# A spectral filter and a maxout feed-forward layer: five visits in the last overlapped batch, and filter rows by way of fp32

## The chip, the cores and the metric

The kernel runs on one core of a Trainium2 chip. The metric is the device time of one execution in microseconds. The core has TensorE (matrix multiplication into PSUM), VectorE, ScalarE, GpSimd, and SyncE, which here only issues DMA transfers. GpSimd issues DMA transfers too.

## The reference

```
x: (8, 3072, 256)   filt_r, filt_i: (1537, 256)

X = rfft(x, axis=1)
y = irfft(X * (filt_r + 1j * filt_i), n=3072, axis=1)      # 8 x 3072 x 256

h1 = y @ w1          # 24576 x 1024
h2 = y @ w2
out = maximum(h1, h2) @ w_out
```

## The kernel before, in words

The transform over 3072 points is split into 96 x 32. A batch passes through four spectral stages: `s1` (a transform of length 96, into `ad` in DRAM, read back as `bt` by `s1_read`), `s2` (twiddles and the transform of length 32, into PSUM tiles `px`), the product with the filter `F` (`product`, tiles `pq`), `s3` (the inverse of length 32, PSUM tiles `pz`, evicted by ScalarE as `zt` and written to `zd` in DRAM, read back as `zr` by `z_read`) and `s4` (the inverse of length 96, giving `yt`). The feed-forward layer then works on tiles of 384 tokens, eight to a batch. It uses max(h1, h2) = max(h1 - h2, 0) + h2: `moe_h` multiplies by `Wd` = w1 - w2 into a PSUM tile `ph`, which VectorE or ScalarE evicts through a maximum with zero as `gt`; `moe_o` sums `gt` times `Wo` and `yt` times `M` = w2 w_out into `po`, evicted by VectorE as `ot` and written out by GpSimd's transfers.

The order is written out by hand. The main loop goes over tiles `tt`, eight steps `j` to each, so 64 steps to a batch. A step issues `moe_h` of this tile, then what the table `mid` holds for the step, then three or four matmul groups of `moe_o` of the tile before, then what the table `todo` holds. While batch b goes through the feed-forward layer, its table entries carry the spectral stages of batch b + 1 (and `s1` of b + 2 in the same visits). `mid` holds the visits: visit n of a batch does `s3` of part n - 1 (there are six parts), `s2` of part n and its two products on VectorE. `plan_f2` puts seven visits into each batch; for batches 2 to 6 they stand at steps 7, 14, 18, 24, 31, 38 and 42, and `z_read` three steps behind the fourth and the seventh. In batch 6 the visits work on the last batch, 7, and carry no `s1`; batch 7 has none. Of each tile VectorE evicts the `ph` of j = 1, 3 and 6, half of the `py` of `s4` and all `po`; ScalarE does the rest.

PSUM tiles `px`, `pz`, `ph`, `py` and `pa` share one pool of six buffers, `ps`, handed out in turn; `po` has two of its own. `pq` has six buffers, `zt` three.

The start-up runs batch 0 through the spectral stages by a path of its own (`s1t`, `t1`, `s3t`, `t2`) and builds the tables. The filter lies in `F`, 128 partitions by real and imaginary part, 12 places w, two s, 256 columns, in bf16. `load_f(h)` fetches the places of half h, in GpSimd's queue behind the eight loads of batch 0's `x`, with a cast from fp32 on the way: rows counted up in partitions 0 to 15 of each half, rows counted down in partitions 16 to 31. For k = 0 the second set is not a row counted down, so row 48 + 96 p comes with a transfer of its own (line 124). `double_f` copies partitions 0 to 31 of each half to 32 to 63: for h = 0 by four VectorE copies (line 130), for h = 1 by SyncE transfers. One row, partition 32 at place 0, is mended by `fix_f` with the last filter row, 1536, which `load_fn` fetches. Only the product of part 0 reads place 0.

Of the kernel before, what the change touches and what calls it, by code (L numbers as in the profile page):

```python
# [8 lines left out]
FP32 = mybir.dt.float32  # L9
# [4 lines left out]
B = 8  # L14
N = 3072
D = 256
# [10 lines left out]
def kernel(  # L27
# [14 lines left out]
    nc = tc.nc  # L42
    V, S, G, TE = nc.vector, nc.scalar, nc.gpsimd, nc.tensor
# [7 lines left out]
    F = const.tile([128, 2, NW, 2, D], BF16)  # L51
# [12 lines left out]
    XF = [const.tile([128, 2, 2, D], FP32, name="XF%d" % k) for k in range(3)]  # L64
# [7 lines left out]
    init = setup.enter_context(tc.tile_pool(name="init", bufs=1))  # L72
# [10 lines left out]
    def load_x(b, c, n):  # L83
        for k in range(c, c + n):
            xb[b, k] = x_tile(b, k)[0:NP]
        src = x[b].rearrange("(p m) d -> p m d", m=NM)
        m0 = 4 * (c % 2)
        G.dma_start(out=xb[b][0:NP, m0:m0 + 4 * n], in_=src[:, 4 * c:4 * c + 4 * n, :])
# [21 lines left out]
    def load_f(h):  # L110
        w0, w1 = WP[h]
        n = 2 * (w1 - w0)
        for g in range(2):
            for ri, f in enumerate((filt_r, filt_i)):
                k0 = 24 * g + 2 * w0
                src = bass.AP(f.tensor, f.offset + k0 * D, [[96 * D, 16], [D, n], [1, D]])
                G.dma_start(out=F[64 * g:64 * g + 16, ri, w0:w1].rearrange("p w s d -> p (w s) d"), in_=src)
                n0 = 1 if k0 == 0 else 0
                src = bass.AP(f.tensor, f.offset + (96 - k0 - n0) * D, [[96 * D, 16], [-D, n - n0], [1, D]])
                G.dma_start(out=F[64 * g + 16:64 * g + 32, ri, w0:w1].rearrange("p w s d -> p (w s) d")[:, n0:n],  # L120
                            in_=src)
                if n0:
                    src = bass.AP(f.tensor, f.offset + 48 * D, [[96 * D, 16], [1, D]])
                    G.dma_start(out=F[16:32, ri, 0, 0], in_=src)

    def double_f(h, g, ri, engine):
        w0, w1 = WP[h]
        o_, i_ = F[64 * g + 32:64 * g + 64, ri, w0:w1], F[64 * g:64 * g + 32, ri, w0:w1]
        if engine is V:
            V.tensor_copy(o_, i_)  # L130
        else:
            nc.sync.dma_start(out=o_, in_=i_)

    FN = init.tile([33, D], FP32)

    def load_fn():
        nc.sync.dma_start(out=FN[32:33], in_=filt_r[1536:1537, :])

    def fix_f():
        V.tensor_copy(F[32:33, 0, 0, 0], FN[32:33])  # L140


    V.memset(W1, 1.0)
# [21 lines left out]
    for q in range(2):  # L165
        G.memset(hv[:, q], 1.0)
        for r in (0, 32):
            G.memset(hv[r:r + 1, q], 0.5 * (1 - q))
    load_f(0)
    load_f(1)  # L170
    load_fn()
    load_x(1, 0, 2)

    def table_c():
# [196 lines left out]
    def s2(b, v):  # L371
        px = [ps.tile([128, 2, D], FP32, tag="ps", name="px%d" % s) for s in range(2)]
        for i in range(2):
            for s, g in ((0, 0), (1, 1), (0, 1), (1, 0)):
                u = 2 * (2 * v + i) + g
                TE.matmul(px[s][64 * g:64 * g + 64, i], U[64 * s:64 * s + 64, u], bt[b][64 * s:64 * s + 64, u],  # L376
                          start=True, stop=True)
        return px

    def product(E, v, s, px, pool=None):  # L380
        pq = (pool or pqpool).tile([128, 2, 2, D], BF16, tag="pq", name="pq")
        E.tensor_tensor(pq, px.rearrange("p (o i) d -> p o i d", o=1).to_broadcast([128, 2, 2, D]),  # L382
                        F[:, :, 2 * v:2 * v + 2, s], OP.mult)
        return pq
# [7 lines left out]
    def s3(b, v, pq):  # L392
        if v == 0:
            zd[b] = dram.tile([NU, 128, D], BF16, tag="zd", name="zd")
        pz = [ps.tile([128, 2, D], FP32, tag="ps", name="pz%d" % g) for g in range(2)]
        for i in range(2):
            for q, tab in enumerate((VP, VQ)):
                for g, s in ((0, 0), (1, 1), (0, 1), (1, 0)):
                    TE.matmul(pz[g][64 * s:64 * s + 64, i], tab[64 * g:64 * g + 64, 2 * v + i, s],  # L399
                              pq[s][64 * g:64 * g + 64, q, i], start=(q == 0), stop=(q == 1))  # L400
        zt = zpool.tile([128, 2, 2, D], BF16, tag="zt", name="zt")
        for g in range(2):
            S.activation(zt[:, :, g], pz[g], AF.Copy)  # L403
        nc.sync.dma_start(out=zd[b][4 * v:4 * v + 4].rearrange("u p d -> p u d"),
                          in_=zt.rearrange("p i g d -> p (i g) d"))

    pend = {}

    def visit(b, n, quads):
# [7 lines left out]
        if n < 6:  # L417
            pend[b, n] = [product(V, n, s, px[s]) for s in range(2)]

    yt = {}  # L420

    def s4(tt):
# [165 lines left out]
    for g in range(2):  # L588
        for ri in range(2):
            double_f(0, g, ri, V)  # L590
            if g == 0 and ri == 0:
                fix_f()
    xs = {}

    def stage_x(v):
# [69 lines left out]
    def plan(b, step, fn, *a):  # L665
        todo.setdefault((b + step // 64, step % 64), []).append((fn, a))
# [6 lines left out]
    mid = {}  # L673

    def plan_f2(b, steps, quads, xs, folds):
        for n, st in enumerate(steps):
            mid.setdefault((b, st), []).append((visit, (b + 1, n, quads[n])))
        plan(b, steps[3] + 3, z_read, b + 1, 0)
        plan(b, steps[6] + 3, z_read, b + 1, 1)
        if b + 2 < B:  # L680
            for c in range(8):
                plan(b, xs[c], load_xf, b + 2, c)
                plan(b, folds[c], fold, b + 2, c)
            plan(b, steps[-1] + (6 if b else 11), s1_read, b + 2)
# [5 lines left out]
    for c in range(2, 8):  # L690
# [1 line left out]
    plan_f1(0, 1, (5, 6, 7, 7, 10, 10, 11, 11, 12, 12, 13, 13), 14)  # L692
    plan_f2(0, (25, 28, 31, 35, 38, 42, 46), ((0,), (1,), (2,), (3,), (4,), (5,), (6, 7)),
            (8, 10, 15, 18, 21, 27, 30, 33), (16, 19, 25, 28, 31, 34, 38, 42))
    for b in range(1, B - 1):
        plan_f2(b, (7, 14, 18, 24, 31, 38, 42) if b > 1 else (14, 18, 24, 30, 34, 39, 42), ((0, 1), (2,), (3,), (4,), (5,), (6,), (7,)),
                range(-32, 32, 8) if b > 1 else range(-25, 31, 7), range(-22, 42, 8) if b > 1 else range(-15, 41, 7))

    for tt in range(8 * B + 1):
        b, i = divmod(tt, 8)  # L700
        k = 0
        for j in range(8):
            step = 8 * i + j
# [4 lines left out]
            if tt > 0:  # L708
                n = 3 if j in (3, 7) else 4
# [36 lines left out]
```

## Time and profile before

| | us |
|---|---|
| median of 3 runs (lowest, highest) | 503.55 (502.16, 515.77) |
| the profiled execution | 502.04 |
| its span, first to last instruction | 500.2 |
| TensorE busy in the span | 488.7 |
| VectorE busy | 331.4 |
| ScalarE busy | 308.6 |
| GpSimd busy | 259.7 |
| mean granted TensorE clock | 0.992 |

Busy time counts instructions in progress; those of TensorE overlap one another, so rows are read from start to start. Times in the views count from the start of the span. "L480" is line 480 of the kernel, and what follows "<-" in brackets is what ended an engine's idle time.

### The profile page before, as it was taken

The page shows a single profiled execution, that of the slowest core. Times are in us where ns is not written, and L with a number is a line of the kernel's source. Part 1 is how long each engine was busy: PE and PEld are TensorE (multiplying, and loading weights), DVE is VectorE, ACT ScalarE, POOL GpSimd, SP SyncE. Part 2 cuts the span into 40 slices and gives each one's busy share as a digit, 9 for nine tenths or more (in the row PEclk, how much of TensorE's full clock was granted, in tenths as well). Part 3 has the DMA queues.
Part 4 walks back from the last instruction along what each step waited for, and adds up shares of the span by engine and source line. Part 5 has one row for each costly group of instructions (what it writes and reads, how often), then busy time and mean ns, then how long its engine had stood idle before and what let it go on. Part 6 is the DMA issues. An engine that isn't in the chain of part 4 may idle for free.

```text
span 500.2 us, 13079 instructions
## 1 busy us (share of the span) xinstructions
PE 488.7 (98%) x5300; PEld 361.7 (72%) x5300; DVE 331.4 (66%) x514; ACT 308.6 (62%) x629; POOL 259.7 (52%) x342
## 2 busy tenths in 40 slices
PE   8699999999999999999999999999999999999996
PEld 4456767777777777777777777777777777777775
DVE  7786788458865786567755787457764687555552
ACT  6777478657764777557674677547774565544442
POOL 7894678548463954627654764637632221222220
PEclk9979999999999999999999999999999999999999
DMA  7999889996899668978789568896759236411112
GB/s 122 166 245 210 260 218 272 294 257 208 234 285 244 180 206 236 240 186 235 206 236 282 178 182 250 222 234 202 201 185 249 84 113 144 167 65 64 64 64 84
DMA packets 77981, 97.19 MB, mean 194 GB/s; under 512 B 8033, under 2 KB 54370, under 8 KB 77858
## 3 DMA queue, kind: packets, MB, share of 16 engines
q1 hardware_dynamic: 64658, 66.73, 51.4%
q0 software_dynamic: 13264, 29.64, 20.5%
q8 instruction: 41, 0.67, 0.6%
q14 instruction: 18, 0.15, 0.1%
HBM read 53.87 MB, written 47.19 MB: 202 GB/s over the span
## 4 chain that ended last, share of the span: by engine, by line
PE 93%; ACT 2%; DMA 1%; DVE 1%; POOL 1%; issue 0%; POOLq 0%
PE po L480 34%; PE ph L448 33%; PE po L478 8%; PE pz L399 5%; PE py L428 4%; PE pa L349 2%; PE px L376 2%; DMA xb<-in_x_dram 1%; PE pt L532 1%; PE pr L553 1%; PE pt L526 1%; PE pa L324 1%; ACT at L509 1%; DVE pq L382 0%; ACT bt L518 0%
## 5 line engine op out<-in xcount | busy, mean ns | idle before, releaser
L480 PE MATMUL po<-Wo,gt 128*128 128x256 bf16 x1536 | 261.0, 273 | 0.0
L452 ACT ACTIVATE gt<-ph 128x384 bf16<-128x384 f32 x321 | 157.2, 496 | 144.9 <-PE ph L448 144.2
L480 PEld LDWEIGHTS <-gt 128*128 128x128 bf16 x1536 | 146.6, 98 | 66.0 <-issue 10.3
L461 POOL DMA_DIRECT2D out_dram<-ot x186 | 103.0, 557 | 171.5 <-DVE ot L492 168.9
L450 DVE TENSOR_SCALAR gt<-ph 128x384 bf16<-128x384 f32 x191 | 105.0, 554 | 64.0 <-PE ph L448 62.0
L382 DVE TENSOR_TENSOR pq<-px,F 128x1024 bf16<-128x1024 f32 x91 | 107.0, 1220 | 23.3 <-PE px L376 22.7
L448 PEld LDWEIGHTS <-Wd 128*128 128x128 bf16 x1024 | 96.5, 98 | 12.1 <-issue 0.5
L103 POOL TENSOR_TENSOR xb<-XF 128x512 bf16<-128x512 f32 x48 | 61.3, 1276 | 53.1 <-PE py L428 24.3
L492 DVE COPY ot<-po 128x512 f32<-128x512 f32 x95 | 65.2, 686 | 25.1 <-PE po L480 24.0
L104 POOL TENSOR_TENSOR xb<-XF 128x512 bf16<-128x512 f32 x48 | 61.1, 1273 | 0.0
L353 ACT ACTIVATE at<-pa 128x512 bf16<-128x512 f32 x96 | 51.8, 608 | 2.4 <-PE pa L349 2.1
L403 ACT ACTIVATE zt<-pz 128x512 bf16<-128x512 f32 x84 | 45.6, 594 | 11.8 <-PE pz L399 9.7
L428 PE MATMUL py<-G,zr 96*128 96x96 bf16 x512 | 32.7, 206 | 0.4 <-DVE zr L556 0.3
L428 PEld LDWEIGHTS <-zr 96*128 96x128 bf16 x512 | 28.9, 97 | 3.0 <-DVE zr L556 1.0
L399 PE MATMUL pz<-pq,VP 64*64 64x256 bf16 x336 | 22.2, 281 | 0.1
L376 PE MATMUL px<-bt,U 64*64 64x256 bf16 x384 | 20.2, 277 | 1.2 <-ACT VQ L273 0.7
L399 PE MATMUL pz<-pq,VQ 64*64 64x256 bf16 x336 | 21.0, 269 | 0.0
L399 PEld LDWEIGHTS <-VP 64*64 64x64 bf16 x336 | 9.8, 105 | 13.6 <-issue 13.3
L349 PE MATMUL pa<-xb,CT 64*64 64x512 bf16 x192 | 19.5, 383 | 0.0
L376 PEld LDWEIGHTS <-U 64*64 64x64 bf16 x384 | 10.5, 108 | 4.1 <-issue 3.8
L563 PE MATMUL pd<-W 128*128 128x512 bf16 x28 | 10.2, 488 | 1.5 <-DVE zero L145 1.5
L349 PEld LDWEIGHTS <-CT 64*64 64x64 bf16 x192 | 8.7, 105 | 2.1 <-ACT gt L452 1.2
(429 smaller groups left out, 606.3 us busy)
## 6 DMA issues: line engine op xcount, KB each, us to landing
out_dram<-ot POOLq DMA_DIRECT2D x186, 128.0 KB, 3.5
XF<-in_x_dram SPq DMA_DIRECT2D x96, 192.0 KB, 5.1
ad<-at SPq DMA_DIRECT2D x56, 192.0 KB, 3.7
zd<-zt SPq DMA_DIRECT2D x42, 256.0 KB, 2.6
zr<-zd SPq DMA_DIRECT2D x56, 192.0 KB, 5.0
bt<-ad SPq DMA_DIRECT2D x13, 768.0 KB, 9.8
WS<-in_moe_w_dram SPq DMA_DIRECT2D x4, 512.0 KB, 7.1
xb<-in_x_dram POOLq DMA_DIRECT2D x8, 192.0 KB, 5.9
```

Source lines behind the costliest of these rows:

```text
L103: G.tensor_tensor(t_[:, 0], f[:, 0], f[:, 1], OP.add)
L104: G.tensor_tensor(t_[:, 1], f[:, 0], f[:, 1], OP.subtract)
L353: S.activation(at[:, m0:m0 + 2], pa[g], AF.Copy)
L382: E.tensor_tensor(pq, px.rearrange("p (o i) d -> p o i d", o=1).to_broadcast([128, 2, 2, D]), F[:, :, 2 * v:2 * v + 2, s], OP.mult)
L399: TE.matmul(pz[g][64 * s:64 * s + 64, i], tab[64 * g:64 * g + 64, 2 * v + i, s], pq[s][64 * g:64 * g + 64, q, i], start=(q == 0), stop=(q ...
L428: TE.matmul(py[:, m], zr[b][:, 4 * i + m, 128 * dc:128 * dc + 128], G1, start=True, stop=True)
L448: TE.matmul(ph, Wd[:, dc, 128 * j:128 * j + 128], y_[:, dc], start=(dc == 0), stop=(dc == 1))
L450: V.tensor_scalar(gt[tt][:, j], ph, 0.0, None, OP.max)
L452: S.activation(gt[tt][:, j], ph, AF.Relu)
L461: E.dma_start(out=dst, in_=ot[tt // 2][:, 3 * (tt % 2) + c])
L480: TE.matmul(p_, g_[:, n - 2, blk], Wo[:, n - 2], start=(e == 0), stop=(e == 9))
L492: V.tensor_copy(ot[tt // 2][:, e - 1:e + 1], po[q // 2 % 2])
```

## The change

Batch 6 gets a table of its own, `LAST`, with five visits at steps 7, 13, 21, 29 and 37 in place of seven at 7, 14, 18, 24, 31, 38 and 42. The visits do `s2` of parts 0 and 1; `s3` of 0 and `s2` of 2 and 3; `s3` of 1 and 2 and `s2` of 4; `s3` of 3 and 4 and `s2` of 5; `s3` of 5. The products of a visit's parts follow its `s2`. `z_read` of batch 7 moves from steps 27 and 45 to 24 and 40.

In the start-up, the filter rows that belong to place 0 of the first half (rows 96 p and 96 p + 48, of both parts of the filter) are fetched by SyncE in fp32 into an `XF` tile that is not yet in use, with row 1536 behind them; GpSimd writes the first four sets, cast to bf16, into `F` ahead of its F loads. `load_f` leaves place 0 out and no longer issues line 124. `fix_f` takes row 1536 from the same tile and stands behind the fourth VectorE copy instead of the first.

```diff
         for g in range(2):
+            n0 = 1 if h == 0 and g == 0 else 0
+            k0 = 24 * g + 2 * w0 + n0
             for ri, f in enumerate((filt_r, filt_i)):
-                k0 = 24 * g + 2 * w0
-                src = bass.AP(f.tensor, f.offset + k0 * D, [[96 * D, 16], [D, n], [1, D]])
-                G.dma_start(out=F[64 * g:64 * g + 16, ri, w0:w1].rearrange("p w s d -> p (w s) d"), in_=src)
-                n0 = 1 if k0 == 0 else 0
-                src = bass.AP(f.tensor, f.offset + (96 - k0 - n0) * D, [[96 * D, 16], [-D, n - n0], [1, D]])
-                G.dma_start(out=F[64 * g + 16:64 * g + 32, ri, w0:w1].rearrange("p w s d -> p (w s) d")[:, n0:n],
-                            in_=src)
-                if n0:
-                    src = bass.AP(f.tensor, f.offset + 48 * D, [[96 * D, 16], [1, D]])
-                    G.dma_start(out=F[16:32, ri, 0, 0], in_=src)
+                for r0, o, step in ((0, k0, D), (16, 96 - k0, -D)):
+                    src = bass.AP(f.tensor, f.offset + o * D, [[96 * D, 16], [step, n - n0], [1, D]])
+                    o_ = F[64 * g + r0:64 * g + r0 + 16, ri, w0:w1].rearrange("p w s d -> p (w s) d")
+                    G.dma_start(out=o_[:, n0:n], in_=src)
...
-    FN = init.tile([33, D], FP32)
+    FZ = XF[0][0:33, 0]

     def load_fn():
-        nc.sync.dma_start(out=FN[32:33], in_=filt_r[1536:1537, :])
+        for ri, f in enumerate((filt_r, filt_i)):
+            for q in range(2):
+                src = bass.AP(f.tensor, f.offset + 48 * q * D, [[96 * D, 16], [1, D]])
+                nc.sync.dma_start(out=FZ[16 * q:16 * q + 16, ri], in_=src)
+        nc.sync.dma_start(out=FZ[32:33, 0], in_=filt_r[1536:1537, :])
+
+    def put_fz(ri):
+        G.tensor_copy(F[0:32, ri, 0, 0], FZ[0:32, ri])

     def fix_f():
-        V.tensor_copy(F[32:33, 0, 0, 0], FN[32:33])
+        V.tensor_copy(F[32:33, 0, 0, 0], FZ[32:33, 0])
...
+    load_fn()
+    for ri in range(2):
+        put_fz(ri)
     load_f(0)
     load_f(1)
-    load_fn()
...
+    LAST = (((), (0, 1)), ((0,), (2, 3)), ((1, 2), (4,)), ((3, 4), (5,)), ((5,), ()))
+
+    def visit_last(b, n):
+        for v in LAST[n][0]:
+            s3(b, v, pend.pop((b, v)))
+        px = {v: s2(b, v) for v in LAST[n][1]}
+        for v in px:
+            pend[b, v] = [product(V, v, s, px[v][s]) for s in range(2)]
...
             double_f(0, g, ri, V)
-            if g == 0 and ri == 0:
-                fix_f()
+    fix_f()
...
-    for b in range(1, B - 1):
+    for n, st in enumerate((7, 13, 21, 29, 37)):
+        mid.setdefault((B - 2, st), []).append((visit_last, (B - 1, n)))
+    plan(B - 2, 24, z_read, B - 1, 0)
+    plan(B - 2, 40, z_read, B - 1, 1)
+    for b in range(1, B - 2):
         plan_f2(b, ...
```

## The prediction

> **What bounds the kernel now.** I read the page's busy table and clock row first, then the chain that ended last, and then the timelines of TensorE, VectorE and GpSimd around the two places that the change touches: the start-up (0 to 32 us) and batch 6 (steps 0 to 63, about 388 to 444 us).
>
> ```profile
> PE 488.7 (98%) x5300; PEld 361.7 (72%) x5300; DVE 331.4 (66%) x514; ACT 308.6 (62%) x629; POOL 259.7 (52%) x342
> PE 93%; ACT 2%; DMA 1%; DVE 1%; POOL 1%; issue 0%; POOLq 0%
> ```
>
> TensorE is the bound: 98% busy and 93% of the chain. All else costs time only where it makes TensorE wait. In batch 6 it has no gap. TensorE around the first two visits of batch 6 (start, duration, instructions):
>
> ```profile
> 393.88 0.49 PE L448 MATMUL ph<-y__7128,Wd 128*128 128x384 bf16 x2
> 394.30 0.41 PE L376 MATMUL px<-bt,U 64*64 64x256 bf16 x8
> 394.64 0.50 PE L480 MATMUL po<-Wo,gt 128*128 128x256 bf16 x3
> ...
> 399.78 0.49 PE L448 MATMUL ph<-y__7192,Wd 128*128 128x384 bf16 x2
> 400.20 0.30 PE L399 MATMUL pz<-pq,VP 64*64 64x256 bf16 x4
> 400.33 0.28 PE L399 MATMUL pz<-pq,VQ 64*64 64x256 bf16 x4
> 400.44 0.28 PE L399 MATMUL pz<-pq,VP 64*64 64x256 bf16 x4
> 400.55 0.28 PE L399 MATMUL pz<-pq,VQ 64*64 64x256 bf16 x4
> 400.66 0.39 PE L376 MATMUL px<-bt,U 64*64 64x256 bf16 x8
> 400.98 0.61 PE L480 MATMUL po<-Wo,gt 128*128 128x256 bf16 x4
> ```
>
> Read start to start, since durations overlap. A ph pair normally takes 0.33 us (431.17 to 431.49 in the same view); before a visit it takes 0.42 (399.78 to 400.20). Eight px take 2 x 0.11 = 0.22 at the rate of the pz rows, and 0.32 where the next work is 128 rows wide (400.66 to 400.98). So a visit pays about 0.1 on entering and 0.1 on leaving: 0.2 us of TensorE time.
>
> VectorE in the same stretch:
>
> ```profile
> 394.75 2.36 DVE L382 TENSOR_TENSOR pq<-px,F 128x1024 bf16<-128x1024 f32 x2 [0.55 <-PE px L376]
> 397.03 0.68 DVE L492 COPY ot<-po 128x512 f32<-128x512 f32 x1
> 397.62 1.01 DVE L450 TENSOR_SCALAR gt<-ph 128x384 bf16<-128x384 f32 x2
> 399.22 0.56 DVE L434 TENSOR_SCALAR y__7286<-py 128x384 bf16<-128x384 f32 x1 [0.58 <-PE py L428]
> ```
>
> A product is 1.22 us, the second of a pair 1.14 later; the evictions behind it are next in VectorE's queue. The evictions behind a pair are done at 398.63, and VectorE then waits 0.58 us: that slack, some 0.6 us a visit, hides each pair today.
>
> **Part 1, batch 6: five visits.** Same matmuls, products and evictions; only their places change. Two visits fewer save 2 x 0.2 = 0.4 us of TensorE. Against it, visits 0 and 1 (steps 7 and 13) now queue four products each in one block. Four take 3 x 1.14 + 1.22 = 4.64 us, in which VectorE evicts nothing. I follow the queues from the first visit with the starts above; the second px set moves TensorE 0.22 later.
>
> Products end at 395.97, 397.11, 398.25, 399.39. Behind them stand ot (to 400.0), gt of step 9 (400.47), gt of step 11 (400.93), y (401.4). PSUM pool ps has six buffers handed out in turn: after four px, step 10's ph takes the first px, step 11's the second, step 12's the third, the first py the fourth, and step 13's ph the buffer of step 9's. With 0.1 us for a release to reach TensorE (an estimate from the start gaps of the rows):
> - step 12's ph: due 397.92 + 0.22 = 398.14, free 398.35: stall 0.2.
> - py: due 398.68 + 0.42 = 399.10, free 399.49: stall 0.4.
> - step 13's ph: due 399.02 + 0.8 = 399.8, free 400.57: stall 0.75.
>
> The second visit then needs six buffers at once (two pz, four px); step 11's gt holds one for 0.1 more. TensorE is through at about 402.0, VectorE begins four more products there, and ends them at 406.6; an ot and the gt of step 14 follow, ready at 407.8. Step 18's first po reads that gt (column 6 of the tile before). TensorE gets there at about 405.9: step 14 starts at 402.45, steps last some 0.76, and step 18's ph waits 0.25 for a px buffer. Stall 0.25 + 1.85.
>
> By then VectorE catches up: visits at steps 21, 29 and 37 bring 2, 2 and 0 products, as many as a visit has now, so I cost them at nothing; the cover is the same 0.6 us. The pairs of pz at steps 21 and 29 give ScalarE four zt of about 0.55 us (400.88 to 401.97 for two in its timeline), 1.1 more in a row than now; with about 1 us idle before its gt rows this is hidden, and uncovered it would cost 0.5. The z reads go out at steps 24 and 40 instead of 27 and 45, and are wanted at step 62: nothing.
>
> Sum for batch 6: 0.2 + 0.4 + 0.75 + 0.1 + 0.25 + 1.85 = 3.55, less 0.4: **+3.1 us**. Bounds: the saving alone, -0.4; and, if the two products that each block of four brings early are exposed in full (4 x 1.14 = 4.6) and the 0.6 us of cover fails at steps 21 and 29 as well (1.2), +5.8.
>
> **Part 2, the filter rows.** GpSimd's queue at the start:
>
> ```profile
> 7.34 0.22 POOL L168 MEMSET hv<- 1x1 f32 x2
> 7.58 0.49 POOL L117 DMA_DIRECT2D F<-in_filt_r_dram  x1
> 8.07 0.58 POOL L120 DMA_DIRECT2D F<-in_filt_r_dram  x1
> 8.65 0.49 POOL L124 DMA_DIRECT2D F<-in_filt_r_dram  x1
> 10.00 0.49 POOL L117 DMA_DIRECT2D F<-in_filt_i_dram  x1 [0.86 <-DMA xb<-in_x_dram]
> ```
>
> Removed: two L124 issues, 1.0 us. Added ahead of the first F issue: two 32x256 copies. The nearest GpSimd copies are 0.26 us (48x96) and 1.05 (128x1024); I take 0.35 each, 0.7. They wait for SyncE's rows: SyncE issues five transfers from 0.75 at 0.36 each, done by 2.6; its transfers on the page land 2.6 to 9.8 us later, so at 5.2 to 12.4 against GpSimd's arrival at 7.56. Most likely no wait (16 KB each, where 9.8 is for 768 KB and 2.6 for 256); at worst 4.8 us. Queued behind are all F loads and load_x(1, 0, 2). The fourth issue waits for an x load until 10.0 anyway, which takes up a delay of 0.9 us. VectorE's copies of F begin at 18.43, behind bt; the second F issue, whose rows the first copy needs, moves from 8.07 to about 8.8, and with the longest landing of its line (7.3 us) is there at 16.1, 2.3 early. So: nothing; at worst 12.4 + 0.7 + 0.5 + 7.3 = 20.9, 2.5 late.
>
> The 64 KB travel ahead of x, which is on the chain (6.17 us of DMA from 4.68). At the 122 to 166 GB/s of the page's first two slices that is 0.4 to 0.5 us if all of it delays x, and nothing if the DMA engines are idle, as they are until about 2.3; F issues 0.7 later give some back. I take **+0.2**, from -0.5 to +0.5.
>
> **Part 3, the mended row** moves from between VectorE's first and second F copy to behind the fourth. Its 0.28 us is in the same unbroken run (18.43 to 23.73), so VectorE ends alike: nothing. GpSimd's first product, at 23.91, now waits for it and starts alike. The second set, F loads for h = 1, moves two places up, about 1 us; its SyncE copies and the w loads follow, with their users busy elsewhere: nothing.
>
> Sum: 502.04 (the profiled execution: span 500.2 plus 1.8 around it) + 3.1 + 0.2 = **505.3 us**. That execution lies 0.3% under the shown median of 503.55 and near its lowest, 502.16. A measurement tells about 2% here, 10 us, so I expect no decided difference.
>
> **Rivals.** (a) *The blocks are absorbed*: if releases come quicker or the buffers go round otherwise, only the visits saved count: 502.04 - 0.4 = 501.6, not slower. For it: VectorE is busy 66% over all. Against: the gt of step 14 is behind the second block in a queue that is in order. It decides if that gt is ready by 405.9. 0.15.
>
> (b) *The clock drops.* From 18.0 to 24.6 us TensorE was busy 3.15 of 6.60 us, longest gap 1.54, and from 24.6 to 31.4 the granted clock was 0.53. My 1.85 us stall makes a window almost as thin. 6.8 us at about half clock costs 3.4: 508.7. Against: the work around the stall is dense. 0.10. The Trainium skill, TensorE: Matmul & The Clock Gate, part 1 (what's actually happening), puts the drop to half rate behind an idle window of about 3.4 us; by that rule none comes here and the sum stays 505.3. The trace does not quite agree: its drop came without so long a gap.
>
> (c) *GpSimd waits for the rows*: the 2.5 us late of part 2's worst case, on top of the forecast: 507.8. Against: with the 4.1 us median of the F loads in place of 7.3 the copy is not held up at all. 0.08.
>
> (d) *VectorE stays behind* to step 29: 502.04 + 5.8 + 0.2 = 508.0. 0.07.
>
> (e) *The start gets shorter*, F out of x's way: -0.5 in place of +0.2, 504.6 with part 1 as forecast. 0.05.
>
> **How the numbers follow.** Forecast 0.55 (its own range 503.8 to 506.8, from +1.8 to +4.8); rivals as given, 0.45 in all. The range reaches down to (a) and up to (b): 501.4 to 508.9. Faster than 2% (under 493.5) has no mechanism: 0.02. Slower than 2% (over 513.6) needs (b), (c) and (d) together, or a wait that I don't see: 0.05. Within: 0.93.
>
> **What would show it.** TensorE gaps at steps 12 to 13 released by VectorE's products and gt, and one of 1 to 2.5 us before a po of step 18 released by gt; four switches fewer (two in, two out) at 0.1 each; blocks of four products of 4.6 us; F's first issue at about 8.3 us; first F copy still at about 18.4. Wrong, if batch 6 has no gap, if the gaps exceed 6 us, or if the start-up shifts by over 1 us.

## The result, and the profile after

The changed kernel takes 505.19 us in the median of six runs (504.92 to 506.02), the kernel before 503.22 in the median of its six. The ratio, which leaves out the one disturbed run of before (515.77), is 1.0048, with a 95% interval of 1.0032 to 1.0064: slower by about 2.4 us (1.6 to 3.2), and within 2%. The profiled execution of the changed kernel took 504.92 us, with a span of 503.2.

The page of the changed kernel, busy table, then the chain by engine:

```profile
PE 489.0 (97%) x5300; PEld 362.2 (72%) x5300; DVE 331.2 (66%) x514; ACT 308.8 (61%) x629; POOL 260.1 (52%) x342
PE 89%; DMA 3%; DVE 3%; POOL 2%; issue 1%; ACT 0%; POOLq 0%; DVEq 0%; SPq 0%
```

No engine's busy time grew by more than 0.4 us. What changed is the chain: TensorE has 89% of it where it had 93%, VectorE 3% for 1% (DMA and GpSimd grew too, in the start-up). TensorE's timeline around the first two visits of batch 6 shows where VectorE got in (start, duration, instructions; in brackets the idle time and who ended it):

```profile
393.99 0.63 PE L382 MATMUL px<-bt,U 64*64 64x256 bf16 x16
394.55 0.50 PE L496 MATMUL po<-Wo,gt 128*128 128x256 bf16 x3
...
398.59 0.51 PE L444 MATMUL py<-G,zr 96*128 96x96 bf16 x8
399.12 0.49 PE L464 MATMUL ph<-y__7195,Wd 128*128 128x384 bf16 x2
399.53 0.30 PE L405 MATMUL pz<-pq,VP 64*64 64x256 bf16 x4
...
399.88 0.28 PE L405 MATMUL pz<-pq,VQ 64*64 64x256 bf16 x4
400.18 0.73 PE L382 MATMUL px<-bt,U 64*64 64x256 bf16 x9
401.11 0.41 PE L382 MATMUL px<-bt,U 64*64 64x256 bf16 x7 [0.20 <-DVE y__7303 L450]
401.45 0.28 PE L496 MATMUL po<-Wo,gt 128*128 128x256 bf16 x1
...
404.84 0.49 PE L464 MATMUL ph<-y__7303,Wd 128*128 128x384 bf16 x2
406.70 0.39 PE L496 MATMUL po<-Wo,gt 128*128 128x256 bf16 x2 [1.38 <-DVE gt L466]
```

Start to start, against what the same work takes without a wait: from the first py to step 13's ph it is 0.53 instead of 0.34 (0.19 lost); from the last pz to the first px it is 0.30 instead of 0.11 (0.19); sixteen px with the switch behind them take 1.27 instead of 0.54 by the rates of the kernel before (0.73; the sixteen of the first visit took 0.56); and from step 18's ph to its first po it is 1.86 instead of 0.33 (1.53). Together 2.64 us. VectorE in the same stretch:

```profile
394.45 4.62 DVE L388 TENSOR_TENSOR pq<-px,F 128x1024 bf16<-128x1024 f32 x4 [0.55 <-PE px L382]
398.98 0.68 DVE L508 COPY ot<-po 128x512 f32<-128x512 f32 x1
399.58 1.01 DVE L466 TENSOR_SCALAR gt<-ph 128x384 bf16<-128x384 f32 x2
400.51 0.55 DVE L450 TENSOR_SCALAR y__7303<-py 128x384 bf16<-128x384 f32 x1
400.97 4.61 DVE L388 TENSOR_TENSOR pq<-px,F 128x1024 bf16<-128x1024 f32 x4
405.50 0.68 DVE L508 COPY ot<-po 128x512 f32<-128x512 f32 x1
406.10 1.01 DVE L466 TENSOR_SCALAR gt<-ph 128x384 bf16<-128x384 f32 x2
```

From 394.45 to 407.1 it never idles. Two blocks of four products stand there, and the first gt behind the second block is the one that TensorE waits for until 406.70.

What the three smaller waits are for shows in narrower windows of the same timelines: the last py, the ph of step 13 and the fourth product of the first block, then a px in the middle of the second visit:

```profile
398.89 0.21 PE L444 MATMUL py<-G,zr 96*128 96x96 bf16 x1
399.12 0.49 PE L464 MATMUL ph<-y__7195,Wd 128*128 128x384 bf16 x2
397.85 1.22 DVE L388 TENSOR_TENSOR pq<-px,F 128x1024 bf16<-128x1024 f32 x1
400.64 0.27 PE L382 MATMUL px<-bt,U 64*64 64x256 bf16 x1
```

The eight py keep their pace, from 398.59 to 398.89. It is the ph behind them that is late: it starts 0.05 us after the fourth product's end at 399.07. The px at 400.18, 400.64 and 401.11 start 0.05 us after three evictions that stand behind the first block: the gt of steps 9 and 11 (the pair ends at 400.59, its first at 400.13) and the y (401.06). So each of these waits ends with VectorE: the first with a product, the others with an eviction queued behind a block.

The span grew by 2.9 us. It can be split by the first ph of a tile, whose start each trace gives:

| start of | before | after | difference |
|---|---|---|---|
| tile 0, end of the start-up | 37.50 | 37.18 | -0.3 |
| tile 48, batch 6 begins | 388.31 | 388.00 | -0.3 |
| tile 56, batch 7 begins | 443.60 | 445.48 | +1.9 |
| last ph | 492.52 | 494.40 | +1.9 |
| end of the span | 500.24 | 503.16 | +2.9 |

So the start-up gained 0.3, batch 6 lost 2.19 (57.48 us against 55.29), and 1.0 came behind the last ph, where the instructions of both kernels keep the same distances and only the last output transfers land later. That end is not the schedule's: from the last ph to the end of the span it is 7.72 us before and 8.76 after, but 7.72 in e1 below, with the same visits as after, and 8.39 in e2, with those of before.

### The profile page after: what moved, and what is told of

The parts are those of the page before. It is cut to its first block, busy times and chain, and to the rows that moved or that the text cites. A ratio compares the mean times of both kernels' runs of the same rounds, so it can differ in the third digit from the quotient of the medians.

```text
span 503.2 us, 13084 instructions
## 1 busy us (share of the span) xinstructions
PE 489.0 (97%) x5300; PEld 362.2 (72%) x5300; DVE 331.2 (66%) x514; ACT 308.8 (61%) x629; POOL 260.1 (52%) x342
## 4 chain that ended last, share of the span: by engine, by line
PE 89%; DMA 3%; DVE 3%; POOL 2%; issue 1%; ACT 0%; POOLq 0%; DVEq 0%; SPq 0%
PE po L496 33%; PE ph L464 32%; PE po L494 8%; PE pz L405 5%; PE py L444 4%; PE pa L355 2%; PE px L382 2%; DVE pq L388 2%; DMA xb<-in_x_dram 1%; DMA F<-F 1%; POOL F L121 1%; POOL xb L88 1%; DMA F<-in_filt_i_dram 1%; PE pr L569 1%; PE pa L330 1%
## 5 line engine op out<-in xcount | busy, mean ns | idle before, releaser
L409 ACT ACTIVATE zt<-pz 128x512 bf16<-128x512 f32 x84 | 45.4, 596 | 10.2 <-PE pz L405 7.2
```

## The experiments

My theory: two blocks of four products hold VectorE's queue, which runs in order, and TensorE waits for the evictions behind them. The rivals: the start-up's changes cost the time; VectorE's load or six PSUM buffers at once cost it wherever the blocks stand. Batch 6, from tile 48 to tile 56, has the same length to 0.01 us wherever it is scheduled alike (before, e2 and e7; after and e1), so it can be read from one trace:

| kernel | batch 6, us | against before | ratio of times (95% interval) |
|---|---|---|---|
| before | 55.29 | 0 | |
| after | 57.48 | +2.19 | 1.0048 (1.0032 to 1.0064) |
| e1, batch 6 alone | 57.48 | +2.19 | 1.0040 (1.0027 to 1.0054) |
| e2, start-up alone | 55.29 | 0.00 | 1.0010 (0.9997 to 1.0024) |
| e3, visits at 7, 15, 23, 31, 39 | 55.46 | +0.17 | 0.9997 (0.9985 to 1.0008) |
| e4, gt of step 14 on ScalarE | 56.78 | +1.49 | 1.0035 (1.0022 to 1.0047) |
| e5, second visit at 14 | 55.96 | +0.67 | 1.0012 (1.0000 to 1.0024) |
| e6, visits at 6, 14, 22, 30, 38 | 55.58 | +0.29 | 1.0007 (0.9995 to 1.0019) |
| e7, mending alone | 55.30 | +0.01 | one run only |
| e8, six visits, one block | 55.07 | -0.22 | 0.9983 (0.9971 to 0.9996) |

**e1, batch 6 alone.** The change without its start-up part:

```diff
+    LAST = (((), (0, 1)), ((0,), (2, 3)), ((1, 2), (4,)), ((3, 4), (5,)), ((5,), ()))
...
-    for b in range(1, B - 1):
+    for n, st in enumerate((7, 13, 21, 29, 37)):
+        mid.setdefault((B - 2, st), []).append((visit_last, (B - 1, n)))
+    plan(B - 2, 24, z_read, B - 1, 0)
+    plan(B - 2, 40, z_read, B - 1, 1)
+    for b in range(1, B - 2):
```

> The five visits of batch 6 alone, the start-up as before. My theory (four products in one block hold VectorE's in-order queue, TensorE waits behind it; the start-up's part is a small gain): the start of batch 6 lies where it lay before (388.3 us), batch 6 takes 2.2 us longer (gaps of some 1.5 us before a po of step 18, 0.9 inside the second visit, 0.2 at the py before it, less 0.4 for two visits saved), and the execution takes 2.2 us more than before, about 505.4. Rival (the start-up's changes cost the time, the visits are neutral): less than 1 us more than before.

Batch 6 is 2.19 us longer, with the same gaps as in the changed kernel, and the time rises by 2.0 us (1.4 to 2.7). The theory's numbers hold; the rival's do not.

**e2, the start-up alone.** The change with batch 6's seven visits left as before:

```diff
-    for n, st in enumerate((7, 13, 21, 29, 37)):
...
-    for b in range(1, B - 2):
+    for b in range(1, B - 1):
```

> The filter rows' new way and the moved mending alone, batch 6 with its seven visits as before. My theory: the first feed-forward tile starts at 37.2 us in place of 37.5, and this 0.3 us is kept to the end: 502.9 against 503.2, too little to tell by the times but plain in the trace. Rival (start-up costs the time): 1 to 2 us slower than before.

Tile 0 starts at 37.07 us, and the start of batch 6 lies 0.31 before that of the kernel before. The time, 0.5 us above before (-0.2 to 1.2), is not told from it. The expectation held here, but what follows takes the 0.3 us back as a gain of the change: with the same start-up code, tile 0 starts at 37.78 in e3, 38.42 in e4, 38.43 in e5, 37.66 in e6 and 36.74 in e8. The old start-up gave 37.50 and 37.36 (e1). The seven new ones average 37.61: no difference can be shown, either way.

**e3, the visits behind the gt of j = 6.**

```diff
-    for n, st in enumerate((7, 13, 21, 29, 37)):
+    for n, st in enumerate((7, 15, 23, 31, 39)):
...
-    plan(B - 2, 24, z_read, B - 1, 0)
-    plan(B - 2, 40, z_read, B - 1, 1)
+    plan(B - 2, 26, z_read, B - 1, 0)
+    plan(B - 2, 42, z_read, B - 1, 1)
```

> All of the change, but the visits at steps 7, 15, 23, 31 and 39 in place of 7, 13, 21, 29 and 37, and the z reads two steps later with them: each block now stands behind VectorE's gt of j = 6 and three steps ahead of its next gt. My theory (it matters which evictions stand behind a block): no gap before the po of step 18, the second block costs no more than the first (0.2 us) and up to 0.3 inside the visit; batch 6 takes 0.1 us longer than before (-0.2 to +0.5), the whole about 503.0, like before. Rival (four products or six PSUM buffers at once cost the time wherever they stand): batch 6 still at least 1.5 us longer, the whole 504.5 or more.

Batch 6 is 0.17 us longer. VectorE's timeline in e3 shows the turned order:

```profile
394.98 4.62 DVE L388 TENSOR_TENSOR pq<-px,F 128x1024 bf16<-128x1024 f32 x4 [0.55 <-PE px L382]
...
401.50 0.68 DVE L508 COPY ot<-po 128x512 f32<-128x512 f32 x1
402.10 0.55 DVE L466 TENSOR_SCALAR gt<-ph 128x384 bf16<-128x384 f32 x1
402.64 4.62 DVE L388 TENSOR_TENSOR pq<-px,F 128x1024 bf16<-128x1024 f32 x4
407.18 0.55 DVE L466 TENSOR_SCALAR gt<-ph 128x384 bf16<-128x384 f32 x1
```

An ot and the gt of step 14 are now ahead of the second block, which is as long as ever. The blocks, the number of visits and the buffers asked for at once are the same as in the changed kernel, and 2.0 of the 2.19 us are gone. (The three later visits and the z reads moved by two steps as well; e5 below moves the second visit alone.)

**e4, one eviction on ScalarE.**

```diff
-        if (tt, j) in on_v if tt < 8 else j in (1, 3, 6):
+        if (tt, j) in on_v if tt < 8 else j in (1, 3, 6) and (tt, j) != (49, 6):
```

> All of the change, with one eviction moved: the gt of step 14 of batch 6 goes to ScalarE, so that it no longer stands behind the second block of products. My theory: the gap before the po of step 18 (1.5 us) goes, the gaps at the py and inside the second visit (1.1 us together) stay, batch 6 takes 0.7 us longer than before (0.4 to 1.1) in place of 2.2, the whole about 503.7. Rival (TensorE would wait there for a PSUM buffer or the next eviction anyway): at least 1 us of the gap is back within the next steps, and batch 6 stays 1.8 us or more longer.

It fell between the two: +1.49, where I expected 0.4 to 1.1 and the rival 1.8 or more. The gt wait is gone, and the next eviction behind the block takes its place. TensorE's timeline in e4:

```profile
406.12 0.49 PE L464 MATMUL ph<-y__7303,Wd 128*128 128x384 bf16 x2
406.44 0.38 PE L496 MATMUL po<-Wo,gt 128*128 128x256 bf16 x2
407.51 0.38 PE L494 MATMUL po<-M,y__7195 128*128 128x256 bf16 x2 [0.69 <-DVE ot L508]
```

The first two po of step 18 run at once. The next pair begins a new po buffer, of which there are two, and waits for the ot copy that stands behind the same block. That takes back 0.85 of the 1.53 us (1.07 from po to po instead of 0.22): the rival's mechanism was at work here, if not to the 1 us that it named. I had looked for one thing behind the block; there were two in a row.

**e5, the second visit one step later.**

```diff
-    for n, st in enumerate((7, 13, 21, 29, 37)):
+    for n, st in enumerate((7, 14, 21, 29, 37)):
```

> All of the change, with the second visit alone put one step later, at step 14 in place of 13. moe_h stands ahead of the visit within a step, so the gt of step 14 is now ahead of the second block in VectorE's queue and not behind it; the time between the two blocks hardly changes. My theory (which eviction is behind the block): the gap before the po of step 18 goes at once, some 0.5 us of waiting stays inside the visit and 0.2 to 0.4 ahead of it; batch 6 takes 0.4 us longer than before (0.1 to 0.9) in place of 2.2. Rival (two blocks too close upon each other: VectorE's load): 1.7 us or more, falling slowly with the distance.

+0.67, as expected (0.1 to 0.9). One step of 0.8 us takes away 1.5, two steps (e3) 2.0. VectorE's load does not fall off like that; the order of its queue does.

**e6, every block directly behind a gt.**

```diff
-    for n, st in enumerate((7, 13, 21, 29, 37)):
+    for n, st in enumerate((6, 14, 22, 30, 38)):
```

(the z reads one step later than in the change)

> All of the change, with the visits at steps 6, 14, 22, 30 and 38 (z reads at 25 and 41): every block directly behind the gt of j = 6, with the longest stretch of a tile to VectorE's next gt. My theory: the wait at the py of step 12 goes, the second visit waits at most 0.3; the two visits saved show for the first time: batch 6 takes 0.2 us less than before (-0.4 to +0.1). Rival (a block of four costs some 0.2 to 0.5 wherever it stands): +0.2 to +0.5, like the visits at 7 and 15. In the whole time neither can be told from before (502 to 504).

A miss: +0.29 and not -0.2. The wait behind the py did go, but the second visit still stops in the middle of its px, in e6's timeline of TensorE:

```profile
402.15 0.49 PE L382 MATMUL px<-bt,U 64*64 64x256 bf16 x9
403.10 0.41 PE L382 MATMUL px<-bt,U 64*64 64x256 bf16 x7 [0.46 <-DVE gt L466]
```

It asks for six PSUM buffers eight steps behind the first block, and one is held by a gt that VectorE reaches only at 402.50. The rival was right on this part: a second block costs TensorE waits even in the best places that I tried. With the 0.45 that the visits saved are worth (2.64 of waits less 2.19), they come to 0.62 us in e3 and 0.74 here.

**e7, the mending alone.** In the kernel before:

```diff
             double_f(0, g, ri, V)
-            if g == 0 and ri == 0:
-                fix_f()
+    fix_f()
```

> The kernel before, with the mending of the row alone moved behind VectorE's fourth F copy. In all four traces so far that have it there VectorE's first product starts 5.26 to 5.29 us after the first F copy, in the two that have it behind the first copy 5.80 to 5.82, and the product always starts 0.50 to 0.53 us after the end of the fourth copy. My theory (a product that reads what a copy wrote starts half a us behind it, and the one-row cast hides there): 5.27 here. Rival (the half us is the wait for TensorE's pv that the profile names, and the shorter run comes from the other way of the rows): 5.8 stays, or the idle time grows by what the cast leaves. The first feed-forward tile starts at 37.0 to 37.6 either way, unless the half-clock stretch of the start-up is 10.2 us and not 6.8, as in the last two runs: then at 37.8 to 38.4.

VectorE's run from the first F copy to the first product takes 5.28 us, as the theory has it and not 5.8. Its timeline in e7:

```profile
18.63 4.76 DVE L130 COPY F<-F 32x4096 bf16<-32x4096 bf16 x4
23.43 0.28 DVE L140 CAST F<-FN 1x256 bf16<-1x256 f32 x1
23.91 1.23 DVE L382 TENSOR_TENSOR pq<-px,F 128x1024 bf16<-128x1024 f32 x1 [0.19 <-DVE F L140]
```

The second half of the expectation failed: tile 0 starts at 38.46 us although the half-clock stretch was 6.8 us long. So the clock is not the only thing that moves the start-up from one execution to the next. In this one VectorE idles for 1.92 us ahead of its sixth product, and GpSimd waits 0.70 us for SyncE's F copies; I did not settle which transfer was behind it.

**e8, six visits with one block.** A version that the others pointed to:

```diff
-    LAST = (((), (0, 1)), ((0,), (2, 3)), ((1, 2), (4,)), ((3, 4), (5,)), ((5,), ()))
+    LAST = (((), (0, 1)), ((0,), (2,)), ((1, 2), (3,)), ((3,), (4,)), ((4,), (5,)), ((5,), ()))
...
-    for n, st in enumerate((7, 13, 21, 29, 37)):
+    for n, st in enumerate((6, 18, 24, 31, 38, 42)):
...
-    plan(B - 2, 24, z_read, B - 1, 0)
-    plan(B - 2, 40, z_read, B - 1, 1)
+    plan(B - 2, 27, z_read, B - 1, 0)
+    plan(B - 2, 45, z_read, B - 1, 1)
```

> All of the change, with six visits in place of five: s2 of 0 and 1 at step 6, then s3 of 0 and s2 of 2 at 18, s3 of 1 and 2 and s2 of 3 at 24, and one part each at 31, 38 and 42 (z reads at 27 and 45). One block of four products is left, behind the gt of j = 6, and the next visit comes only when VectorE has caught up; in the run with visits at 6, 14, 22, 30 and 38 the block at step 6 left TensorE without a gap up to step 13. My theory (a visit saved is worth 0.2 us where no block makes TensorE wait): no gap in batch 6, which takes 0.2 us less than before (-0.25 to -0.1). Rival (the price of a visit is not on the chain, or a block costs wherever it stands): 0 or more. In the whole time neither can be told.

Batch 6 takes 0.22 us less than before, without a wait of TensorE: a visit saved is worth its two switches once the only block stands right behind a gt and the next visit comes twelve steps later. The time is below that of before (0.9983, 0.9971 to 0.9996) and well below that of the changed kernel. Of the 0.9 us of the ratio batch 6 explains 0.22; the rest I do not ascribe to the schedule, since the profiled spans are 500.4 and 500.2.

## Why the prediction was right, point by point

The total was close (505.3 predicted, 505.19 measured), and the mechanism was the one forecast. Its terms were less exact than the total, and so was the change itself: +3.3 us forecast, +2.4 (1.6 to 3.2) measured.

- *What bounds*: TensorE, with time lost only where it waits. Right: busy times did not change, the chain did.
- *Saving of 0.4 for two visits*: right. e8 shows 0.22 for one; in the changed kernel 2.64 of gaps less the 2.19 lost leave 0.45.
- *Step 18's po behind the gt of step 14*: right in place and cause, 1.53 us against 1.85.
- *First block, 1.35 us at step 12's ph, the py and step 13's ph*: the mis-sized term. Only step 13's ph lost time, 0.19 in place of 0.75. The forecast gave the four px buffers to the ph of steps 10, 11 and 12 and to the first py, and step 13's ph the buffer of step 9. In the trace the first py starts at 398.59, 0.48 before the fourth product ends, and it is step 13's ph that starts right behind that end (399.12 for 399.07). The ph of step 11 waits for a semaphore of ScalarE, which reads no px. So the px buffers were asked for later than the forecast has it. A release also took 0.05 us to reach TensorE and not 0.1.
- *Second visit, 0.1*, and *step 18's ph, 0.25*: also mis-sized. TensorE reached the second visit earlier than forecast and lost there 0.92 (0.19 and 0.73) to the evictions behind the first block, and at step 18's ph nothing. Together with the first block the terms other than the po came to 1.7 us in the forecast and 1.11 on the chip.
- *Later visits at nothing*: right. TensorE has no gap in the visits at 21 and 29.
- *Start-up +0.2*: not decided. The profiled pair shows -0.3, the other new start-ups spread from 36.74 to 38.43 us. The first F copy, forecast at about 18.4, starts at 17.60 in the changed kernel and at 18.19 to 19.01 in the other six new start-ups. Two details are clear. GpSimd's copies took 0.54 each, not 0.35, and did not wait for SyncE's rows; the first F issue came at 8.65:

```profile
7.62 1.08 POOL L141 CAST F<-XF 32x256 bf16<-32x256 f32 x2
8.65 1.33 POOL L121 DMA_DIRECT2D F<-in_filt_r_dram  x2
```

- *Mending moved, nothing*: wrong in size for VectorE, whose run got 0.5 us shorter (5.29 for 5.82, shown by e7), and right in its effect on tile 0, as far as the spread lets one see.
- *Rival (a), absorbed*: refuted by 2.64 us of gaps. *(b), a clock drop*: did not come; in the window of the gap the granted clock (the figure behind POOL's) stayed at 1.00, with TensorE busy 0.62 of 2.00 us:

```profile
405.00:407.00 2.00, 0.62 (x5) 0.28 (x4) 2.00 (x4) 0.49 (x1) 0.53 (x1) 1.00 0.00 0
```

  The Trainium skill, TensorE: Matmul & The Clock Gate (Part 1, what's actually happening), asks for an idle window of about 3.4 us before the rate is halved; here its rule gave the better forecast than my reading of the start-up, where the drop did come behind a longest gap of 1.54 us. *(c), rows late*: GpSimd went on without a wait. *(d), VectorE behind to step 29*: it had caught up by step 20, where it waits for the py of step 20 with 0.82 us idle. *(e), a shorter start*: not decided, as said above.

That the sum came so close is in good part luck. In the profiled execution batch 6 was 0.9 us cheaper than forecast, the start 0.5 earlier, and the end 1.0 later, which no term had foreseen. And the sum started from an execution of 502.04, 1.2 us under the median of before (503.22), which makes up for the 0.9 us that the forecast change had too much.

## What to carry to other kernels

When work is gathered into fewer and larger blocks to save switches, price what stands behind the block in the queue of the engine that runs it, item by item, and look for the first of these that the bounding engine needs: here a switch saved was worth 0.1 us and a block one step too early 1.5. If a block must be, put it right behind the last item that is needed soon and let the queue run empty before the next one (e8). And take away one wait only after asking what waits next behind the same block (e4).

## What the runs showed of the hardware that was not expected

A product that reads what VectorE's own copies wrote starts 0.50 to 0.53 us behind the end of the last copy, in all ten traces (before, after, e1 to e8), wherever the one-row cast stands. The profile of the kernel before names a matmul as what ended that wait, but the px that this product reads were through at 22.1 us (their last row starts at 21.71 and takes 0.41). With the cast in between, the wait hides it: that is what the shorter run of e7 rests on. Why the product starts so late, the traces do not show. The four lines of the kernel before, against those of e7 above:

```profile
18.43 1.22 DVE L130 COPY F<-F 32x4096 bf16<-32x4096 bf16 x1
19.68 0.28 DVE L140 CAST F<-FN 1x256 bf16<-1x256 f32 x1
20.00 3.73 DVE L130 COPY F<-F 32x4096 bf16<-32x4096 bf16 x3
24.25 1.23 DVE L382 TENSOR_TENSOR pq<-px,F 128x1024 bf16<-128x1024 f32 x1 [0.52 <-PE pv L259]
```

The half-clock stretch of the start-up lasts 6.8 us in seven of the ten traces and 10.2 in three (e3, e4 and e6, with the same start-up code as after, e2, e5 and e8). The windows of 4 us of the kernel before, then of e3 (busy time of PE, PEld, DVE, ACT and POOL, then the granted clock):

```profile
22.00:26.00 4.00, 1.94 (x88) 1.11 (x82) 3.48 (x4) 3.19 (x7) 3.94 (x3) 0.78 0.85 161
26.00:30.00 4.00, 4.00 (x79) 2.30 (x81) 4.00 (x4) 2.12 (x6) 4.00 (x3) 0.50 0.95 248
30.00:34.00 4.00, 3.89 (x120) 2.20 (x118) 3.33 (x4) 3.74 (x8) 4.00 (x5) 0.87 0.99 351
```

```profile
18.00:22.00 4.00, 2.43 (x98) 1.65 (x97) 3.94 (x4) 3.78 (x9) 3.62 (x4) 0.92 0.98 126
22.00:26.00 4.00, 2.15 (x88) 1.17 (x81) 3.78 (x5) 2.90 (x6) 3.94 (x4) 0.50 0.83 158
26.00:30.00 4.00, 4.00 (x83) 2.17 (x75) 4.00 (x5) 2.45 (x5) 4.00 (x3) 0.50 1.00 316
30.00:34.00 4.00, 3.89 (x112) 2.28 (x108) 2.58 (x4) 3.49 (x7) 4.00 (x4) 0.80 0.82 305
```

At half rate a window of 4 us shows 0.50, so 0.78 stands for 1.8 us at half rate and 0.87 for 1.0: 6.8 us with the full window. In e3 it is 0.6 + 4 + 4 + 1.6 = 10.2. That is two and three times 3.4 us. The Trainium skill, TensorE: Matmul & The Clock Gate (Part 1, what's actually happening), gives the gate a free-running window of about 3.4 us; the lengths agree with it. The profiles do not show which event decides between two and three.
